# A gated recurrence and a feed-forward block on one core: the first chunk's hand-written order exchanged for another

## The chip, the core and the metric

One Trainium2 chip, one of its cores. A core has TensorE (PE, with weight loads shown as PEld), VectorE (DVE), ScalarE (ACT), GpSimd (POOL) and SyncE (SP), which here issues nearly all DMAs. Each engine runs its own instructions in order and waits on semaphores for the others. The metric is the device time of one execution in microseconds, lower is better.

## The reference

An mLSTM cell over 4 batches x 8 heads x 768 steps with head size 40, then a feed-forward block. At each step, with stabilised input and forget gates `i`, `f`:

```python
C = f * C + i * outer(v, k)        # state, 40 x 40 a head
n = f * n + i * k
y = sigmoid(o) * (C @ q) / max(abs(n @ q), 1)
```

The outputs of all heads are put side by side, `x` of 3072 tokens x 320, and then `out = leaky_relu(x @ w_in, 0.01) @ w_out` with 2048 inner columns. `w_in` and `w_out` come as fp64, all else as fp32.

## The kernel before

The 768 steps are cut in 6 chunks of 128; a chunk has 4 samples (one for each batch), numbered `s` = 4 * chunk + batch. Within a chunk the recurrence is written as attention: scores k q^T, a decay mask's exponential, the product with v, and a state carried on. Then the chunk's 512 tokens go through the feed-forward block.

**Chunk 0 (`first_chunk`)** is ordered by hand. The text `ORDER` is a list of steps with arguments, and each step appends its instructions to the engines' queues in that order (`tc.manual_schedule` keeps it for PE, DVE, ACT and POOL; SP's DMAs follow the order of the calls too). The steps that matter here:

- `warm n`: n matmuls of the identity into a bank that nobody reads, 128x128 fp32. The trace has two records for each.
- `g c`, `ge c`, `ug c`: a chunk's gate sums on DVE (L297 to L317), their exponentials on ACT (L323 to L329), and turning them on PE (`tg`, copied at L357 and L359).
- `ld s`, `lo s`, `fd s`, `ll s i`, `lw n`: loads. `ld` is k, q and v of a sample; `lo` its output gate; `fd` k, v and the decay rows of a sample of chunk 1 (L375, L382, L451); `ll` q or the gate (L422); `lw n` one weight piece, 0 to 3 quarters of `w_in` (each in four requests, L231), 4 and up an eighth of `w_out` (L237).
- `tr s i`, `tc s i`: turn k (0) or q (1) on PE (L586), copy it on ACT (L592). `sc`, `scm`: scores on PE (L601), times the decay on DVE (L608). `ab n`, `abw s`: decay rows of two samples on PE (L472), with the mask on DVE (L482). `exp`: eight exponentials on ACT (L499).
- `vu`, `st`, `stc`: v times gate on POOL (L509), state sum on PE (`dC`, L616), copied on DVE (L624). `val`, `den`, `o`, `gate`, `gp`: values on PE (`pa`, L681), denominators (L673 to L675), tanh on ACT (L534), gating on DVE (L693), scaling on POOL (L710). `x`, `xc`: turn the result (L884) and copy it (L897, L898).
- `nw n e`: the next step of narrowing weight piece n (half e, if given) from fp64 to fp32: a cast on ACT (L264) and six steps on DVE (L266, L268, L270, L275, L279, L281). The last writes the weights that the matmuls read.
- `ff j b0 b1`: one feed-forward unit of some samples (`ph`, L915), with its leaky relu on ACT (L923).
- `tiles`, `ps n`: fills of GpSimd. 

PSUM is 8 banks: 4 for feed-forward and fillers (tag "mm"), 4 for the cell (tag "c"); a step that opens a bank waits for the readers of the one that it takes. SP's DMAs share eight landing semaphores, so an issue waits until the DMA eight places ahead has landed.

**The rest of chunk 0's feed-forward** is a loop over 30 units `ffs[i]`: units 0 and 1 finish the two tiles for samples 2 and 3, 2 to 13 are the other tiles of `x @ w_in` (two units a tile), 14 to 29 multiply by `w_out` (L951; four steps of accumulation for each of 4 samples). Between them:

- `PASSES[i]`: how many steps of the other narrowing (pieces 2 to 11, seven steps each) are put ahead of unit i.
- `fetch`: ahead of which unit a piece of `w_out` is loaded (n = 3 to 7).
- `place`: after which unit the next entry of chunk 1's list of cell work is put: `u_parts` (`sd`, L658 and L663) and `u_plain` (`hN`, L721) of samples 4 to 7, the gates of chunk 2, four turnings.
- `ahead(s)`, called ahead of unit 0 for sample 4 and after each `u_plain` for the next one: turns k and q (`u_split`, PE `tk` at L559, ACT copies at L567), scales q (L527), carries the state (L636) and scales k (`vu`, L519), the last three on POOL.

After these units a planner's table drives chunks 1 to 5; the change doesn't touch it.

Of the kernel before, what the change touches and what calls it, by code (L numbers as in the profile page):

```python
# [22 lines left out]
def kernel(  # L23
# [27 lines left out]
    B, H, S, D = q.shape  # L51
# [25 lines left out]
    gp = ctx.enter_context(tc.tile_pool(name="gates", bufs=1))  # L77
# [67 lines left out]
    def subs(s):  # L145

        for u in range(2):
            yield u, ts(u, SL), slice(SL * (1 - u), SL * (1 - u) + D)
# [212 lines left out]
    st = {}  # L361
# [44 lines left out]
    def padded(s):  # L406

        return rb_t[s % NR][:, 1, : H * DP].rearrange("p (h d) -> p h d", d=DP)
# [8 lines left out]
    def load_late(s, i):  # L417

        if B <= s < 2 * B:
            if i > 0:  # L420
                c, b = divmod(s, B)
                nc.sync.dma_start(natural(s, i), (k, q, o_gate)[i][b, :, ts(c, P), :].rearrange("h p d -> p h d"))  # L422
        elif s < NS:
            load_blocks(s, i)
# [28 lines left out]
    def spread_q(s):  # L453

        c, b = divmod(s, B)
        d = st.setdefault(s, {})
        d["ea"] = late_t[:, s % EAB, :].rearrange("p (h t) -> p h t", t=SL)
        for r in range(2):
            nc.sync.dma_start(
                d["ea"][ts(r, SL)], a_dr[c, 1, 1 - r, b * H : (b + 1) * H, :].partition_broadcast(SL),  # L460
            )
# [24 lines left out]
    def prep_mask(s):  # L486
        if s in masked:
            return
        masked.add(s)
        w = st[s]["w"]  # L490
        nc.gpsimd.tensor_tensor(w, w, cm2.unsqueeze(1).to_broadcast([P, H, SL]), op=ALU.add)  # L491

    def prep_exp(s):

        c, b = divmod(s, B)
        w = st[s]["w"]
        for h in range(H):
            bh = b * H + h
            yield nc.scalar.activation(w[:, h, :], w[:, h, :], AF.Exp, bias=gT[c][:, 0, bh : bh + 1], scale=1.0)  # L499
# [23 lines left out]
    def prep_qs(s):  # L523

        c, b = divmod(s, B)
        d = st[s]
        nc.gpsimd.tensor_tensor(  # L527
            mixed(s)[:, 0, :, :D], natural(s, 1), gT[c][:, 2, ts(b, H)].unsqueeze(2).to_broadcast([P, H, D]), op=ALU.mult,
        )
# [10 lines left out]
    def prep_kq(s):  # L540

        d = st[s]
        d["kqT"] = cw.tile([P, 2, PR * P], F32, name="kqT")
        for i in range(2):
            nc.vector.transpose(
                d["kqT"][:, i].rearrange("p (h t n) -> p h n t", n=TS, t=QW),
                raw_blocks(s, i, QW).rearrange("p (h n) d -> p h n d", n=TS),
            )
        for r in range(2):
            rows = ts(r, SL)  # L550
            nc.vector.tensor_tensor(  # L551
                mixed(s)[rows, 1 - r], d["kqT"][rows, 1].rearrange("p (h t) -> p h t", t=SL), d["ea"][rows], op=ALU.mult,
            )

    def turned(name, src):

        bank = psc.tile([P, PR, P], F32, name=name, tag="c")
        for j in range(PR):
            nc.tensor.transpose(bank[:, j, :], src[:, 2 * j : 2 * j + 2, :].rearrange("p h d -> p (h d)"), ident[:])  # L559
        return bank  # L560

    def to_halves(s, bank, dst):

        for u, toks, rows in subs(s):
            by = dst(u, rows).rearrange("p (j e) t -> p j e t", e=2)
            for e in range(2):
                nc.scalar.copy(by[:, :, e, :], bank[DP * e : DP * e + D, :, toks])  # L567
# [2 lines left out]

        to_halves(s, turned("tq", mixed(s)[:, 0]), lambda u, rows: mixed(s)[rows, u])

    def u_split(s):

        d = st[s]
        d["kqT"] = cw.tile([P, 2, PR * P], F32, name="kqT")
        for i, bank in enumerate([turned("tk0", d["k"]), turned("tk1", padded(s))]):
            to_halves(s, bank, lambda u, rows: d["kqT"][rows, i].rearrange("p (h t) -> p h t", t=SL))

    def u_transpose(s, i):  # L580
        d = st[s]
        if i == 0:
            d["kqT"] = cw.tile([P, 2, PR * P], F32, name="kqT")
        tp = d["tp", i] = psc.tile([P, PR, P], F32, name="tkq", tag="c")
        for j in range(PR):
            nc.tensor.transpose(  # L586
                tp[:, j, :], d["kq"[i]][:, 2 * j : 2 * j + 2, :].rearrange("p h d -> p (h d)"), ident[:],
            )
# [42 lines left out]
    def state_next(s, u):  # L631
        c, b = divmod(s, B)
        rows, old = state_of(s, u)
        _, new = state_of(s, 1 - u)
        g = gL[c][rows, u, ts(b, H)].unsqueeze(2).unsqueeze(3).to_broadcast([D, H, 2, V1])
        nc.gpsimd.tensor_tensor(new, old, g, op=ALU.mult)  # L636
# [442 lines left out]
    def ahead(s):  # L1079

        if s < NS:
            if s < 2 * B:
                u_split(s)
            if s >= 2 * B:
                late[s] = 3
            lazy[s] = prep_exp(s)
            if s < 2 * B:
                prep_qs(s)
            else:
                prep_kq(s)  # L1090
            if s + NR < NS:
                load_late(s + NR, 0)
                load_late(s + NR, 1)
                if s + NR >= 2 * B:
                    spread_q(s + NR)
            state_next(s, 0)
            if s >= 2 * B:
                place_v(s)
            prep_vu(s)
            if s + 1 <= 2 * B:  # L1100
                prep_mask(s + 1)
# [10 lines left out]
            nc.tensor.matmul(st["warm"][:], lhsT=ident[:], rhs=ident[:], start=True, stop=True)  # L1112

    ORDER = """
warm 2; warm 2; g 0; ld 1; ld 0; ge 0; lo 0; ld 2
lw 0; lo 1; warm 6; warm 5; ab 0; ug 0; tr 1 0; tr 0 0
tc 1 0; ld 3; lo 2; tr 0 1; abw 1; abw 0; warm 1; tc 0 1
tc 0 0; tr 1 1; sc 0; warm 3; vu 1; vu 0; lw 1; lo 3
st 0; o 0; tc 1 1; exp 0; scm 0; exp 1; stc 0; st 1
stc 1; warm 5; warm 1; sc 1; warm 6; scm 1; val 0; ab 2  # L1120
g 1; abw 2; abw 3; tr 2 0; tc 2 0; o 1; tr 2 1; val 1
warm 1; tr 3 0; vu 2; ps 1; ge 1; nw 0 0; den 0; gate 1
gate 0; tc 2 1; vu 3; tiles; tc 3 0; exp 2; o 2; warm 5
sc 2; gp 0; den 1; scm 2; nw 0 1; nw 0 0; nw 0 0; ug 1
warm 2; warm 1; nw 0 0; nw 0 1; x 0; tr 3 1; val 2; nw 0 1
warm 4; st 2; xc 0; tc 3 1; exp 3; gate 2; den 2; sc 3
stc 2; gp 1; scm 3; x 1; gp 2; ps 0; fd 4; nw 0 0
nw 0 0; nw 0 1; st 3; ll 4 1; lw 2; warm 5; val 3; nw 0 1
nw 0 0; xc 1; o 3; gate 3; den 3; nw 0 1; nw 0 1; nw 1
nw 1; stc 3; nw 1; ps 3; nw 1; ll 4 2; lw 3; x 2  # L1130
warm 1; ff 0 0 2; gp 3; ps 2; fd 5; ll 5 1; lw 4; x 3
xc 2; xc 3; lw 5; fd 6; fd 7; nw 1; nw 1; ff 1 0 2
ll 5 2; lw 6; nw 1
"""

    def first_chunk():

        ffs, narrow = [], {}

        def ff(j, b0, b1):  # L1140
            if not ffs:
                ffs.extend(ff_units(0))
            ffs[0](j, b0, b1)

        def step(n, e=None):
            if (n, e) not in narrow:
                narrow[n, e] = narrow_weights(n, e)
            next(narrow[n, e], None)

        acts_of = {  # L1150
            "ld": load, "lo": load_o, "lw": load_weights, "g": gates, "ge": gates_exp, "warm": warm,
            "ug": lambda c: gates_T(c, bus[c][0] if c == 0 else bus.pop(c)[0]),
            "tr": u_transpose, "tc": transpose_copy, "ab": lambda n: spread_first(bus[0][1], n), "abw": spread_mask,
            "exp": lambda n: run(prep_exp(n)), "vu": prep_vu, "tiles": prepare_tiles, "sc": u_scores, "scm": scores_mix,
            "st": state, "stc": state_copy, "val": u_values, "den": values_den, "o": prep_o, "gate": gate,
            "gp": gate_scale, "nw": step, "ps": prepare_step, "x": u_x, "xc": x_copy, "ff": ff,
            "warmer": warmer, "idle": idle, "fd": feed, "ll": load_late,
        }
        for line in ORDER.split("\n"):
            for what in line.split(";"):  # L1160
                name, *args = what.split() or [None]
                if name:
                    acts_of[name](*map(int, args))
        return ffs[1]

    E = mybir.EngineType
    with tc.manual_schedule(engines={E.PE, E.DVE, E.Activation, E.Pool}):
        ffs = first_chunk()
        fetch = {1: (3, 4), 16: (7,), 12: (5, 6)}
        PASSES = (6, 0, 3, 0, 3, 3, 0, 3, 0, 2, 1, 0, 5, 1, 11, 0, 1, 3, 3, 3, 1, 12, 2, 3, 4, 0, 2, 1, 2, 21)  # L1170
        place = (1, 6, 11, 12, 16, 18, 19, 20, 22, 23, 25, 25, 26)
        late = {}
        now = (None for n in range(2, QN + NF // 2) for _ in narrow_weights(n))

# [9 lines left out]
        for i in range(len(ffs)):  # L1184
            run(now, PASSES[i])
            for n in fetch.get(i, ()):
# [13 lines left out]
            while done < min(len(cells), sum(p <= i for p in place)):  # L1200
                fn, s = cells[done]
# [7 lines left out]
            while fed < done:  # L1209
                fn, s = cells[fed]  # L1210
# [134 lines left out]
```

## Time and profile before

| | us |
|---|---|
| median of 3 runs | 484.05 |
| lowest, highest | 483.19, 484.30 |
| the profiled execution | 484.15 |
| its span, first to last instruction | 482.3 |
| PE, DVE, ACT, POOL busy | 475.2, 363.9, 199.5, 161.3 |
| first feed-forward matmul starts | 38.91 |
| chunk 1's feed-forward starts | 129.63 |

Times in the trace count from the span's start; what lies around the span is 484.15 - 482.3 = 1.85 us. A row of the timeline gives start, length, engine, line, operation, tiles out<-in, shape and count; in brackets stands how long the engine was idle before it and who released it. Matmul ends are modelled, so TensorE can seem busy while it waits for a short time.

### The profile page before, as it was taken

How to read it: one execution, taken by the hardware profiler on the slowest of the kernel's cores; microseconds unless marked ns; L12 is line 12 of the kernel's file. 1: busy time of each engine (PE TensorE's matmuls, PEld its weight loads, DVE VectorE, ACT ScalarE, POOL GpSimd, SP SyncE). 2: the span in 40 equal slices, each digit the busy share in tenths (PEclk: the TensorE clock that was granted, in tenths of full speed). 3: DMA queues.
4: the chain of work that ended last, by engine and by line, in shares of the span. 5: the costliest groups of instructions: out<-in, count | busy, mean ns of one | idle time of the engine just before them, and what ended most of it. 6: DMA issues, size and time to landing. Idle time of an engine off the chain costs nothing.

```text
span 482.3 us, 12095 instructions
## 1 busy us (share of the span) xinstructions
PE 475.2 (99%) x4757; PEld 373.6 (77%) x4757; DVE 363.9 (75%) x601; ACT 199.5 (41%) x523; POOL 161.3 (33%) x209
## 2 busy tenths in 40 slices
PE   8999999989999999999999999999999999999997
PEld 7998755767655499955569985548998899988997
DVE  4589997999917989877897957889899967335611
ACT  3597875662732332305251222624025642156310
POOL 4056132462602827545641644562310002000020
PEclk9999999999999999999999999999999999999999
DMA  8989868885536676676767968754150030100001
GB/s 146 209 151 223 206 95 246 228 209 123 127 100 130 151 168 168 158 178 175 153 170 161 229 162 207 174 138 121 64 224 31 1 110 0 51 6 1 7 8 41
DMA packets 142599, 63.35 MB, mean 131 GB/s; under 512 B 110480, under 2 KB 130768, under 8 KB 142544
## 3 DMA queue, kind: packets, MB, share of 16 engines
q1 hardware_dynamic: 142160, 62.47, 54.5%
q8 instruction: 37, 0.61, 0.5%
q14 instruction: 18, 0.15, 0.1%
q10 hardware_dynamic: 384, 0.13, 0.1%
HBM read 51.68 MB, written 8.27 MB: 124 GB/s over the span
## 4 chain that ended last, share of the span: by engine, by line
PE 86%; DVE 7%; DMA 2%; SPq 1%; POOL 1%; ACT 1%; issue 1%; POOLq 0%; DVEq 0%
PE po L990 32%; PE ph L915 25%; PE ph L841 8%; PE po L951 4%; PE pe L841 4%; PE pT L751 3%; PE sd L658 3%; PE warm L340 3%; DVE w_out L281 1%; DMA raw<-in_moe_w_out_dram 1%; PE sd L663 1%; DMA S<-in_v_dram 1%; DVE late L270 1%; DVE w_out L279 1%; PE pa L681 1%
## 5 line engine op out<-in xcount | busy, mean ns | idle before, releaser
L915 PE MATMUL ph<-xT,w_in 64*128 64x512 f32 (+1 forms) x680 | 142.4, 569 | 0.4 <-DVE w_in L281 0.3
L915 PEld LDWEIGHTS ph<-xT,w_in 64*128 64x128 f32 x680 | 68.4, 187 | 63.9 <-issue 60.0
L990 PE MATMUL po<-w_out,acts 128*128 128x160 f32 x640 | 90.2, 300 | 0.0
L990 PEld LDWEIGHTS po<-w_out,acts 128*128 128x128 f32 x640 | 87.4, 190 | 1.9 <-ACT w L499 0.8
L923 ACT ACTIVATE acts<-ph 128x512 f32<-128x512 f32 (+1 forms) x68 | 35.1, 567 | 79.1 <-PE ph L915 79.0
L499 ACT ACTIVATE w<-w,gT 128x64 f32<-128x64 f32 (+1 forms) x192 | 51.7, 347 | 28.1 <-POOL w L491 28.1
L636 POOL TENSOR_TENSOR S<-S,f 40x336 f32<-40x336 f32 x36 | 35.0, 973 | 76.5 <-PE pT L751 50.9
L990 PE MATMUL po<-raw,acts 128*128 128x160 f32 x320 | 45.1, 299 | 0.0
L1028 POOL TENSOR_TENSOR y<-y,raw 128x160 f32<-128x160 f32 x10 | 6.3, 633 | 113.3 <-ACT y L1027 113.3
L990 PEld LDWEIGHTS po<-raw,acts 128*128 128x128 f32 x320 | 44.0, 190 | 0.0
L668 DVE TENSOR_TENSOR qn<-w,sd 64x512 f32<-64x512 f32 x40 | 27.4, 685 | 20.5 <-PE sd L663 12.2
L951 PE MATMUL po<-w_out,acts 128*128 128x320 f32 x128 | 36.5, 436 | 0.0
L863 DVE SCALAR_TENSOR_TENSOR acts<-ph,acts 128x512 f32<-128x512 f32 x32 | 20.6, 685 | 20.6 <-ACT acts L861 20.6
L551 DVE TENSOR_TENSOR qn<-kqT,late 64x512 f32<-64x512 f32 x32 | 35.0, 1093 | 1.0
L491 POOL TENSOR_TENSOR w<-w,i 128x512 f32<-128x512 f32 x20 | 31.8, 1588 | 9.3 <-ACT acts L923 9.2
L951 PEld LDWEIGHTS po<-w_out,acts 128*128 128x128 f32 x128 | 23.6, 190 | 9.7 <-issue 0.8
L765 POOL TENSOR_TENSOR xb<-xb,den 128x320 f32<-128x320 f32 x16 | 11.7, 729 | 47.5 <-DVE xb L762 47.5
L861 ACT ACTIVATE acts<-pe 128x512 f32<-128x512 f32 x32 | 17.4, 594 | 18.6 <-PE pe L841 18.6
L769 DVE STREAM_TRANSPOSE x<-xb 128x512 f32<-128x512 f32 x16 | 17.8, 1109 | 7.8 <-POOL xb L765 7.8
L658 PEld LDWEIGHTS sd<-kqT 40*64 40x64 f32 x640 | 19.7, 135 | 5.0 <-issue 4.6
L867 ACT ACTIVATE acts<-acts 128x512 f32<-128x512 f32 x32 | 19.7, 633 | 8.2 <-DVE acts L863 8.2
L990 PE MATMUL po<-raw 128*128 128x160 f32 x160 | 22.8, 300 | 0.0
(167 smaller groups left out, 774.9 us busy)
## 6 DMA issues: line engine op xcount, KB each, us to landing
w<-a_dr SPq DMA_DIRECT2D x40, 128.0 KB, 3.7
rb<-in_k_dram SPq DMA_DIRECT2D x64, 80.0 KB, 2.6
rb<-in_q_dram SPq DMA_DIRECT2D x64, 80.0 KB, 2.5
rb<-in_o_gate_dram SPq DMA_DIRECT2D x64, 80.0 KB, 2.5
xT<-x_dr SPq DMA_DIRECT2D x32, 160.0 KB, 3.4
late<-a_dr SPq DMA_DIRECT2D x32, 128.0 KB, 3.1
x_dr<-x SPq DMA_DIRECT2D x16, 256.0 KB, 2.6
kn<-in_k_dram SPq DMA_DIRECT2D x24, 160.0 KB, 3.8
```

The costliest lines, as they stand in the source:

```text
L491: nc.gpsimd.tensor_tensor(w, w, cm2.unsqueeze(1).to_broadcast([P, H, SL]), op=ALU.add)
L499: yield nc.scalar.activation(w[:, h, :], w[:, h, :], AF.Exp, bias=gT[c][:, 0, bh : bh + 1], scale=1.0)
L551: nc.vector.tensor_tensor(mixed(s)[rows, 1 - r], d["kqT"][rows, 1].rearrange("p (h t) -> p h t", t=SL), d["ea"][rows], op=ALU.mult,)
L636: nc.gpsimd.tensor_tensor(new, old, g, op=ALU.mult)
L658: nc.tensor.matmul(bank[1 - u][toks, h, :], lhsT=kqT[rows, 0, ts(h, SL)], rhs=kqT[rows, 1, ts(h, SL)], start=True, stop=True,)
L668: nc.vector.tensor_tensor(mixed(s)[toks, u], w[toks], bank[1 - u][toks], op=ALU.mult)
L841: nc.tensor.matmul(ph[r][:], lhsT=parts["w", key][n][part, at : at + P], rhs=xs[key][part, slot, :], start=start and slot == 0, stop=stop ...
L863: nc.vector.scalar_tensor_tensor(fs[r], in0=ph[r][:], scalar=1.0 + EPS, in1=fs[r], op0=ALU.mult, op1=ALU.add,)
L915: nc.tensor.matmul(ph[r][:, cols], lhsT=w_row(r, slot, j), rhs=xT[DP * r : DP * (r + 1), slot, bs, :], start=(slot == 0), stop=(slot == KC ...
L923: nc.scalar.activation(acts[:, f, cols], ph[r][:, cols], AF.Prelu, alpha=0.01)
L951: nc.tensor.matmul(po[n][:], lhsT=acts[:, f, ts(n, P)], rhs=w_out[:, f, :], start=(f == 0), stop=(f == NF - 1),)
L990: nc.tensor.matmul(bank[:], lhsT=left[:, f, :], rhs=right[:, f, :], start=f == 0, stop=f == KH - 1)
```

## The change

Four things change, and no arithmetic:

1. `u_split` is cut in two, `split_turn` (PE) and `split_copy` (ACT). For sample 4 they become steps of `ORDER` (`sp 4`, `spc 4`, close to its end), and `ahead` skips them for that sample.
2. `ORDER` is another text: the same steps otherwise, with 44 fillers instead of 50, in another order. On SP, `lw 0` stands ahead of `ld 2`, `lo 3` ahead of `lw 1`, `lw 4` ahead of `fd 5`, and `fd 7` last.
3. `fetch` loads pieces 3 and 4 of `w_out` ahead of unit 3 instead of 1, and 5 and 6 ahead of unit 7 instead of 12.
4. `PASSES` and `place` have other numbers: sample 4's and sample 5's `u_plain` one unit later (7 and 13), sample 6's `u_parts` and `u_plain` one unit earlier (15 and 17), the turnings at 23, 24, 24, 27 instead of 23, 25, 25, 26.

```diff
--- before.py
+++ after.py
@@ -570,12 +570,21 @@
 
         to_halves(s, turned("tq", mixed(s)[:, 0]), lambda u, rows: mixed(s)[rows, u])
 
+    def split_turn(s):
+
+        st[s]["tk"] = [turned("tk0", st[s]["k"]), turned("tk1", padded(s))]
+
+    def split_copy(s):
+
+        d = st[s]
+        d["kqT"] = cw.tile([P, 2, PR * P], F32, name="kqT")
+        for i, bank in enumerate(d.pop("tk")):
+            to_halves(s, bank, lambda u, rows: d["kqT"][rows, i].rearrange("p (h t) -> p h t", t=SL))
+
     def u_split(s):
 
-        d = st[s]
-        d["kqT"] = cw.tile([P, 2, PR * P], F32, name="kqT")
-        for i, bank in enumerate([turned("tk0", d["k"]), turned("tk1", padded(s))]):
-            to_halves(s, bank, lambda u, rows: d["kqT"][rows, i].rearrange("p (h t) -> p h t", t=SL))
+        split_turn(s)
+        split_copy(s)
 
     def u_transpose(s, i):
         d = st[s]
@@ -1079,7 +1088,7 @@
     def ahead(s):
 
         if s < NS:
-            if s < 2 * B:
+            if B < s < 2 * B:
                 u_split(s)
             if s >= 2 * B:
                 late[s] = 3
@@ -1112,25 +1121,25 @@
             nc.tensor.matmul(st["warm"][:], lhsT=ident[:], rhs=ident[:], start=True, stop=True)
 
     ORDER = """
-warm 2; warm 2; g 0; ld 1; ld 0; ge 0; lo 0; ld 2
-lw 0; lo 1; warm 6; warm 5; ab 0; ug 0; tr 1 0; tr 0 0
-tc 1 0; ld 3; lo 2; tr 0 1; abw 1; abw 0; warm 1; tc 0 1
-tc 0 0; tr 1 1; sc 0; warm 3; vu 1; vu 0; lw 1; lo 3
-st 0; o 0; tc 1 1; exp 0; scm 0; exp 1; stc 0; st 1
-stc 1; warm 5; warm 1; sc 1; warm 6; scm 1; val 0; ab 2
-g 1; abw 2; abw 3; tr 2 0; tc 2 0; o 1; tr 2 1; val 1
-warm 1; tr 3 0; vu 2; ps 1; ge 1; nw 0 0; den 0; gate 1
-gate 0; tc 2 1; vu 3; tiles; tc 3 0; exp 2; o 2; warm 5
-sc 2; gp 0; den 1; scm 2; nw 0 1; nw 0 0; nw 0 0; ug 1
-warm 2; warm 1; nw 0 0; nw 0 1; x 0; tr 3 1; val 2; nw 0 1
-warm 4; st 2; xc 0; tc 3 1; exp 3; gate 2; den 2; sc 3
-stc 2; gp 1; scm 3; x 1; gp 2; ps 0; fd 4; nw 0 0
-nw 0 0; nw 0 1; st 3; ll 4 1; lw 2; warm 5; val 3; nw 0 1
-nw 0 0; xc 1; o 3; gate 3; den 3; nw 0 1; nw 0 1; nw 1
-nw 1; stc 3; nw 1; ps 3; nw 1; ll 4 2; lw 3; x 2
-warm 1; ff 0 0 2; gp 3; ps 2; fd 5; ll 5 1; lw 4; x 3
-xc 2; xc 3; lw 5; fd 6; fd 7; nw 1; nw 1; ff 1 0 2
-ll 5 2; lw 6; nw 1
+warm 6; warm 2; warm 2; g 0; ld 1; ld 0; ge 0; lo 0
+lw 0; ld 2; lo 1; warm 5; ab 0; tr 0 0; tr 1 0; tc 1 0
+ld 3; lo 3; lo 2; tr 0 1; abw 0; abw 1; tc 0 1; tc 0 0
+tr 1 1; ug 0; sc 0; vu 0; vu 1; lw 1; warm 5; warm 4
+st 0; st 1; o 0; tc 1 1; exp 0; scm 0; exp 1; stc 0
+sc 1; warm 4; scm 1; stc 1; val 0; ab 2; nw 0 0; g 1
+tr 2 0; val 1; tc 2 0; o 1; tr 2 1; tr 3 0; ps 1; vu 2
+ge 1; abw 2; abw 3; den 1; den 0; gate 1; gate 0; tc 2 1
+tc 3 0; vu 3; exp 2; gp 0; o 2; warm 4; ug 1; sc 2
+scm 2; nw 0 1; nw 0 0; nw 0 0; warm 2; nw 0 0; nw 0 1; x 0
+tr 3 1; val 2; nw 0 1; warm 4; st 2; xc 0; tc 3 1; exp 3
+den 2; gate 2; st 3; sc 3; stc 2; gp 1; gp 2; tiles
+ps 0; fd 4; nw 0 1; nw 0 0; scm 3; x 1; ll 4 1; lw 2
+warm 4; nw 0 0; nw 0 1; warm 2; nw 0 0; xc 1; o 3; val 3
+nw 0 1; gate 3; den 3; nw 1; stc 3; ps 3; ff 0 0 2; ll 4 2
+lw 3; x 2; nw 0 1; nw 1; nw 1; nw 1; gp 3; ps 2
+lw 4; fd 5; ll 5 1; x 3; xc 2; xc 3; lw 5; fd 6
+nw 1; nw 1; nw 1; ff 1 0 2; lw 6; ll 5 2; sp 4; spc 4
+fd 7
 """
 
     def first_chunk():
@@ -1154,7 +1163,7 @@
             "exp": lambda n: run(prep_exp(n)), "vu": prep_vu, "tiles": prepare_tiles, "sc": u_scores, "scm": scores_mix,
             "st": state, "stc": state_copy, "val": u_values, "den": values_den, "o": prep_o, "gate": gate,
             "gp": gate_scale, "nw": step, "ps": prepare_step, "x": u_x, "xc": x_copy, "ff": ff,
-            "warmer": warmer, "idle": idle, "fd": feed, "ll": load_late,
+            "sp": split_turn, "spc": split_copy, "warmer": warmer, "idle": idle, "fd": feed, "ll": load_late,
         }
         for line in ORDER.split("\n"):
             for what in line.split(";"):
@@ -1166,9 +1175,9 @@
     E = mybir.EngineType
     with tc.manual_schedule(engines={E.PE, E.DVE, E.Activation, E.Pool}):
         ffs = first_chunk()
-        fetch = {1: (3, 4), 16: (7,), 12: (5, 6)}
-        PASSES = (6, 0, 3, 0, 3, 3, 0, 3, 0, 2, 1, 0, 5, 1, 11, 0, 1, 3, 3, 3, 1, 12, 2, 3, 4, 0, 2, 1, 2, 21)
-        place = (1, 6, 11, 12, 16, 18, 19, 20, 22, 23, 25, 25, 26)
+        fetch = {7: (5, 6), 16: (7,), 3: (3, 4)}
+        PASSES = (6, 0, 4, 0, 5, 2, 0, 1, 2, 1, 1, 1, 3, 1, 7, 1, 2, 1, 4, 6, 1, 12, 0, 5, 6, 1, 1, 0, 1, 21)
+        place = (1, 7, 11, 13, 15, 17, 19, 20, 22, 23, 24, 24, 27)
         late = {}
         now = (None for n in range(2, QN + NF // 2) for _ in narrow_weights(n))
 
```

More of the change, by code (lines that the diff above doesn't have):

```diff
@@ L571, in split_qs, with u_split @@
         to_halves(s, turned("tq", mixed(s)[:, 0]), lambda u, rows: mixed(s)[rows, u])
-    def u_split(s):
+    def split_turn(s):
+        st[s]["tk"] = [turned("tk0", st[s]["k"]), turned("tk1", padded(s))]
+    def split_copy(s):
         d = st[s]
         d["kqT"] = cw.tile([P, 2, PR * P], F32, name="kqT")
-        for i, bank in enumerate([turned("tk0", d["k"]), turned("tk1", padded(s))]):
+        for i, bank in enumerate(d.pop("tk")):
             to_halves(s, bank, lambda u, rows: d["kqT"][rows, i].rearrange("p (h t) -> p h t", t=SL))
+    def u_split(s):
+        split_turn(s)
+        split_copy(s)
     def u_transpose(s, i):
```

## The prediction

> **What bounds the kernel now.** First the top of the page, then the busy time by stage (columns: PE, PEld, DVE, ACT, POOL busy with counts, PE clock, DMA share, GB/s).
>
> ```profile
> span 482.3 us, 12095 instructions
> ...
> PE 475.2 (99%) x4757; PEld 373.6 (77%) x4757; DVE 363.9 (75%) x601; ACT 199.5 (41%) x523; POOL 161.3 (33%) x209
> ```
>
> ```profile
> 84.35:107.48 23.13, 21.91 (x241) 16.09 (x239) 21.95 (x35) 14.65 (x42) 11.93 (x11) 1.00 0.88 219
> ...
> 129.63:483.00 353.37, 349.33 (x3571) 277.68 (x3570) 252.94 (x400) 115.73 (x301) 106.30 (x128) 1.00 0.45 114
> ```
>
> TensorE is busy for all but 7 us. From 129.63 us to the end the same instructions stand in the same order in both kernels; those 353 us move as a block. So the question is how much earlier TensorE reaches 129.63. After its start at 1.47 it is idle for little, as its waits show (us in total, times, longest):
>
> ```profile
> PE tg L347 <- DVE hn L732: 0.7, 1, 0.7
> ...
> PE sd L663 <- POOL vu L519: 0.5, 1, 0.5
> PE ph L915 <- DVE w_in L281: 0.3, 1, 0.3
> ```
>
> But "busy" hides two things. Ahead of 38.91 it runs 50 fillers (`warm`, matmuls of the identity that nothing reads), which pass time until others are done. And VectorE is almost as full: 21.95 of 23.13 us from 84.35 on. It narrows the fp64 weights, and TensorE waits for it wherever the order lets it fall behind. Three places carry the sum: the end of the front, chunk 0's third weight quarter, and the two stalls after 100 us.
>
> **The change part by part.** Nothing is added to the arithmetic. There are 44 fillers instead of 50; all else is order.
>
> *The front to sample 1's values.* The chain (start, length, what):
>
> ```profile
> 16.41 1.09 PE sc L601 x16
> 17.50 1.53 PE warm L340 x12
> 19.03 1.71 PE pa L681 x16
> 20.75 1.10 PE ab L472 x32
> ...
> 41.93 2.43 PE ph L915 x20
> 44.36 1.02 PE tk L559 x8
> ```
>
> VectorE there (start, length; brackets: idle before, and who ended it):
>
> ```profile
> 14.88 1.29 DVE L608 TENSOR_TENSOR w<-w,sc 128x512 f32<-128x512 f32 x2 [2.75 <-ACT w L499]
> ...
> 21.95 0.28 DVE L305 TENSOR_TENSOR a<-F,m 32x128 f32<-32x128 f32 x1 [2.09 <-PE ab L472]
> ...
> 26.07 1.29 DVE L693 SCALAR_TENSOR_TENSOR x<-acts,pa 128x320 f32<-128x320 f32 x2 [0.35 <-ACT kqT L592]
> ...
> 28.08 1.28 DVE L608 TENSOR_TENSOR w<-w,sc 128x512 f32<-128x512 f32 x2 [0.27 <-ACT w L499]
> ...
> 33.07 0.68 DVE L624 COPY S<-dC 40x168 f32<-40x168 f32 x2 [0.19 <-PE dC L616]
> 34.21 1.29 DVE L608 TENSOR_TENSOR w<-w,sc 128x512 f32<-128x512 f32 x2 [0.46 <-ACT w L499]
> ...
> 40.54 1.24 DVE L281 SCALAR_TENSOR_TENSOR w_in<-w_in,late 128x640 f32<-128x640 f32 x1
> ...
> 42.56 0.68 DVE L624 COPY S<-dC 40x168 f32<-40x168 f32 x2
> ```
>
> The exponentials on ScalarE stand behind the same four copies and one tanh as before, so I leave them where they are; sample 0's mix on VectorE then still ends at 14.88 + 1.29 = 16.17. In the new order that mix frees the banks of sample 1's scores, which start at about 16.17 instead of 16.41: 0.24 earlier. Behind them stand 4 fillers instead of 6; twelve records (six fillers) took 1.53, so one takes 0.255 and two are worth 0.51. Values 0 (1.71) and ab 2 (1.10) follow as now. So L305, which waits for ab 2, goes from 21.95 to 21.2: **0.75 earlier**. If ScalarE were late instead, these 0.75 go; if TensorE could run freely here, all six fillers (1.53) would be won.
>
> *From L305 to the second feed-forward unit.* VectorE takes from 21.95 to 40.54 + 1.24 = 41.78 to reach the end of the first quarter's second half (L281), which `ff 1` waits for; the brackets in between sum to 0.35 + 0.27 + 0.19 + 0.46 = 1.27 idle. The new order holds the same steps. Followed step by step with the durations of the trace, VectorE waits only for the scores of sample 2, about 0.3. The bounds are 0 and 1.27; I take 0.97 won. Against that, the state copy of sample 3 (0.68 at 42.56) now stands ahead of this L281 instead of behind it. So it ends at 41.78 - 0.75 - 0.97 + 0.68 = 40.74, and `ff 1` starts **1.04 earlier**. TensorE is there in time: `ff 0` needs the half that ends 1.72 earlier, at about 37.2, then come 2.43 for `ff 0` and 0.68 for two turnings, 40.3. VectorE itself, with the copy done, is 1.72 ahead.
>
> *The turning of chunk 1's first k and q (tk, 1.02 at 44.36).* On TensorE it stands directly behind `ff 1` in both orders: worth nothing. On ScalarE its eight copies now stand ahead of the cast of quarter 2 instead of behind it; that cast then ends at about 48.7, just when VectorE comes for it (50.70 - 1.72 = 48.98, from the first row below). Nothing gained; if VectorE were earlier still, it would wait there.
>
> ```profile
> 49.21 1.49 DVE L281 SCALAR_TENSOR_TENSOR w_in<-w_in,late 128x1280 f32<-128x1280 f32 x1
> ...
> 58.91 1.48 DVE L281 SCALAR_TENSOR_TENSOR w_in<-w_in,late 128x1280 f32<-128x1280 f32 x1
> ```
>
> ```profile
> 51.59 11.79 PE L915 MATMUL ph<-xT,w_in 64*128 64x512 f32 x52
> ...
> 65.40 10.57 PE L915 MATMUL ph<-xT,w_in 64*128 64x512 f32 x48
> ...
> 84.35 6.73 PE L951 MATMUL po<-w_out,acts 128*128 128x320 f32 x24
> ```
>
> *Third quarter.* 48 passes take 10.57, so 0.22 each; the 52 from 51.59 should take 11.45 and take 11.79. The 0.34 are a wait: after 40 passes (60.4) TensorE stood before quarter 2's L281, which ends at 58.91 + 1.48 = 60.39. New: TensorE is there at 50.55 + 8.8 = 59.35, L281 done at 58.67. The wait goes: **0.34**, and VectorE keeps 0.7 in hand.
>
> *Sample 4's plain part one unit later, samples 5 and 6 shifted.* Here a new wait can arise. VectorE has five steps of w_out's first load ahead of sample 4's gate, and GpSimd's chain behind that gate ends in `vu` of sample 5, which the `sd` matmuls at 76.49 (now 75.1) need:
>
> ```profile
> 65.15 1.94 DVE L281 SCALAR_TENSOR_TENSOR w_in<-w_in,late 128x1280 f32<-128x1280 f32 x1
> ...
> 72.60 1.23 DVE L281 SCALAR_TENSOR_TENSOR w_out<-w_out,xb 128x640 f32<-128x640 f32 x1
> ...
> 77.92 1.40 DVE L668 TENSOR_TENSOR qn<-w,sd 64x512 f32<-64x512 f32 x2 [2.41 <-ACT qn L567]
> ...
> 79.77 0.81 DVE L270 SCALAR_TENSOR_TENSOR late<-w_out,late 128x640 uint16<-128x640 uint16 x1
> 80.50 0.48 DVE L275 TENSOR_SCALAR w_out<-w_out 128x640 uint32<-128x640 uint32 x1
> ```
>
> ```profile
> 68.91 0.74 POOL L710 TENSOR_TENSOR x<-x,den 128x320 f32<-128x320 f32 x1 [3.17 <-DVE x L732]
> ...
> 71.97 1.19 POOL L519 TENSOR_TENSOR vu<-kn,gT 128x320 f32<-128x320 f32 x1
> ```
>
> Quarter 3's L281 ends at 67.09, now 65.37. From there to the end of the load's L281 the trace needs 73.83 - 67.09 = 6.74, gate included; its L281 (1.23) moves behind the gate. So the gate is done by 70.9, GpSimd starts 0.14 later and needs 4 instructions, 68.91 to 73.16, 4.25: 75.3. Late by 0.2 at most, and queued behind it on TensorE is everything. I add **0.2**. In the other direction: VectorE idles 2.41 ahead of 77.92, and two steps that now follow (0.81 and 0.48) are put into that idle time, which gives VectorE 1.3 more lead.
>
> *The two stalls after 100 us.* TensorE waits 0.7 for sample 6's gate and 0.5 for sample 7's `vu` behind it.
>
> ```profile
> 97.03 1.21 PE L721 MATMUL hN<-S,qn 128*64 128x42 f32 x32
> ```
>
> ```profile
> 100.81 0.16 DVE L673 TENSOR_SCALAR den<-hN 128x8 f32<-128x8 f32 x1
> ```
>
> Sample 6's hN ends at 98.24, but VectorE takes up its denominators 2.6 later, at 100.81, because load 8's other steps and two of load 9's stand ahead. In the new order one step of load 8 stands ahead of them and five follow, and the whole part comes one w_out unit earlier (24 passes in 6.73 are three units, 2.24 each). Gate and `vu` then come over 3 us sooner against TensorE than now; both stalls go: **1.22**. What is late next is load 9's L281, about 1 us ahead of its matmul.
>
> *Transfers.* On SP the first quarter's four requests pass sample 2's three loads:
>
> ```profile
> 8.00 0.80 SPq L373 DMA_DIRECT2D kn<-in_k_dram  x1
> ...
> 10.58 2.80 SPq L231 DMA_DIRECT2D acts<-in_moe_w_in_dram  x4
> ```
>
> ```profile
> DMA to landing us min/median/max: 3.2/6.8/7.6
> ```
>
> They are issued 10.58 - 8.00 = 2.58 earlier and land, at 7.6 after the last issue, by 18; the cast that reads them stands behind exponentials that end at 17.5, with 3 us of room to the next turning. Sample 2's loads come about 2.8 later, by 18 to 20.4, and are turned at 21 or later. The loads of w_out that move (4 ahead of sample 5's, 5 and 6 from unit 12 to 7) arrive before their casts. I cost all of it at nothing; each us of lateness at the first cast beyond 20.5 would cost that much.
>
> **Sum:** -1.04 - 0.34 + 0.2 - 1.22 = -2.4 us. The profiled execution took 484.15 us with a span of 482.3, so 481.75; the median of the three runs is 484.05, 0.1 below it, so **481.7**. About 0.2% (1 us) is what a measurement of this kernel can tell from no change.
>
> **Rivals.** *The stalls move instead of going.* GpSimd or VectorE falls behind at sample 5, 6 or 7, since steps on VectorE vary with what GpSimd does beside them (0.48 and 0.82 to 1.3 for like steps). Then 1.22 is lost and 1.2 remain: 482.9. For it: margins of 0 to 1 us. Against: over 3 us at the stalls themselves. 0.17.
>
> *The front gains nothing.* If the first cast or the mixes keep VectorE's pace, and the stalls only shrink, -0.3 to -0.9 remain: about 483.5. 0.11.
>
> *The clock falls (slower).* At the start thirty filler records ran slowly:
>
> ```profile
> 1.47 6.46 PE L340 MATMUL warm<-ident 128*128 128x128 f32 x30 [1.47 <-POOL ident masks.py:199]
> ```
>
> ```profile
> 9.04:12.17 3.13, 0.46 (x2) 1.00 1.12 195
> ```
>
> 6.46 for thirty, against 30 x 0.1275 = 3.83 at the later rate. In the new order the front has four groups of turnings in a row and a wait for the copies, about 9.04 to 11.75, with no matmul at all; if TensorE's clock falls there and is not back until ab 2, its work up to that point (scores 2 x 1.09, fillers 13 x 0.255, values 1.71, ab 1.10, states 0.74) takes twice as long, up to 9.0 us more, of which the waits there absorb little: 484.1 - 2.4 + 9.0 = 490.7. From 2.4 us of such loss on, the kernel is slower. Against it: now from 9.04 to 12.17 the only matmul is one filler (0.46 of 3.13), and what follows runs at full rate. The Trainium skill ("TensorE: Matmul & The Clock Gate", Part 4: PE-mode transpose, and Part 1) says that transposes don't count as busy and that about 3.4 us idle halve the clock; by it 2.7 us would pass, and one window lost would cost some 2.6. The trace's 3.13 us agree that this is short enough. 0.05.
>
> Further unforeseen collisions of queues: 0.07, half of them slower.
>
> **How the numbers follow.** Forecast 0.6, the rivals 0.17, 0.11, 0.05, the rest 0.07. Faster by over 0.2%: 0.6 + 0.17 + a few of the third = 0.79. Within 0.2%: 0.11. Slower: 0.10, the clock and half of the rest, rounded up for what a hand schedule misses. The range: down to 480.2 (all 1.27 idle and all fillers of the front won), up to 483.7 (front without gain); beyond lie the clock and part of the rest.
>
> **What would show it.** `ff 1` at about 40.9, quarter 1's L281 done at 49.0, `sd` of sample 5 near 75.1 with no wait for `vu`, w_out's first unit near 83, no TensorE wait at sample 6's gate, and 129.63 becoming 127.2. Wrong: a TensorE wait over 0.5 on `vu`, or fillers at the slow rate after 9 us.

## The result, and the profile after

Over 12 executions each, the median went from 483.88 us (482.87 to 484.73) to 481.72 us (480.94 to 483.62). The ratio is 0.9966, 95% interval 0.9951 to 0.998: faster by 0.2 to 0.5%. The recorded 481.7 is met, but the 12 executions fall into two groups, and that was not foreseen: seven at 480.94 to 481.74 with a mean TensorE clock of 1.000, five at 483.1 to 483.62 with 0.996. The profiled execution (483.1 us, span 481.1) is one of the five. (Apart from these groups, a few executions of several kernels, of the kernel before too, took several us or far longer, all but one, the 2776.31 of `later_half`, with a mean clock of 0.993 or less; the counts of falls leave them out.) Its page, the totals and the slices:

```profile
span 481.1 us, 12080 instructions
...
PE 474.7 (99%) x4745; PEld 373.6 (78%) x4745; DVE 365.4 (76%) x601; ACT 199.7 (42%) x523; POOL 160.4 (33%) x209
...
PEclk9998999999999999999999999999999999999999
```

The fourth digit of the clock's row, the slice from 36.1 to 48.1 us, is below 9. Cut into the stretches around it (columns as in the prediction's first table; the clock stands third from the end):

```profile
34.26:37.67 3.41, 2.90 (x26) 2.69 (x26) 3.41 (x6) 2.71 (x5) 2.26 (x8) 1.00 0.99 208
37.70:41.11 3.41, 3.41 (x19) 2.91 (x16) 3.28 (x9) 0.00 (x0) 1.90 (x6) 0.50 1.07 223
41.11:44.52 3.41, 3.41 (x29) 2.53 (x28) 3.34 (x4) 3.07 (x9) 3.33 (x3) 1.00 1.18 194
```

From 37.70 to 41.11 us TensorE gets half its clock. The chain there shows what stands in that stretch:

```profile
33.32 1.50 PE L340 MATMUL warm<-ident 128*128 128x128 f32 x12
34.66 2.17 PE L690 MATMUL pa<-S,w 128*128 128x41 f32 x16
37.24 4.12 PE L924 MATMUL ph<-xT,w_in 64*128 64x256 f32 x20 [0.41 <-DVE w_in L281]
...
42.09 2.43 PE L924 MATMUL ph<-xT,w_in 64*128 64x256 f32 x20
```

The first feed-forward unit starts at 37.24, 1.67 earlier than before (38.91), but its 20 passes take 4.12 instead of 2.43, and the second unit starts at 42.09 instead of 41.93. Against the kernel before, TensorE's waits are now these (us in total, times, longest):

```profile
PE sc L610 <- ACT kqT L601: 0.5, 1, 0.5
PE po L960 <- DVE w_out L281: 0.5, 1, 0.5
PE ph L924 <- DVE w_in L281: 0.4, 1, 0.4
```

The two after 100 us are gone, as forecast; a new one of 0.5 stands at w_out (120.3 us), and one of 0.5 at the first scores. The next chunk's feed-forward starts at 128.38 (129.63 before), 1.25 earlier in spite of the lost clock.

The same kernel profiled once more, without a fall (`again`, below; 481.23 us, span 479.3):

```profile
34.17 2.17 PE L690 MATMUL pa<-S,w 128*128 128x41 f32 x16
36.75 2.43 PE L924 MATMUL ph<-xT,w_in 64*128 64x256 f32 x20 [0.41 <-DVE w_in L281]
...
40.12 2.43 PE L924 MATMUL ph<-xT,w_in 64*128 64x256 f32 x20
```

Here the second unit starts at 40.12 and the next chunk's at 126.66, 2.97 ahead of before. Not all of that is the change: executions also differ at their start. The same 18 records of fillers, first in the profiled execution of after, then in `again`:

```profile
4.19 3.51 PE L340 MATMUL warm<-ident 128*128 128x128 f32 x18
```

```profile
4.18 2.33 PE L340 MATMUL warm<-ident 128*128 128x128 f32 x18
```

At 0.213 a record while slow and 0.112 when fast, with 0.16 behind the last, 13 of the 18 were slow in the first (up to 7.0 us) and 1.5 in the second (up to 4.5). The profiled execution of before had its slow rate until 7.5, the latest of all here. So the lengths of stretches are compared, not times from zero. From the PE and ScalarE timelines: the start of sample 0's exponentials (L499), from there to the second feed-forward unit, from that to w_out's first unit, from that to the next chunk's feed-forward:

| kernel (one profile each) | exp. start | to 2nd unit | to w_out | to chunk 1 |
|---|---|---|---|---|
| before | 12.69 | 29.24 | 42.42 | 45.28 |
| after, clock falls | 12.24 | 29.85 | 41.87 | 44.42 |
| again (after, no fall) | 11.76 | 28.36 | 42.10 | 44.44 |
| fill2_again | 12.07 | 28.36 | 42.11 | 44.43 |
| front_half | 11.54 | 29.21 | 42.41 | 45.27 |
| later_half | 11.53 | 29.19 | 42.79 | 44.43 |
| split_only | 12.52 | 29.25 | 42.41 | 45.28 |
| unit6 | 12.04 | 28.37 | 42.10 | 44.42 |
| queue | 11.73 | 29.69 | 42.12 | 44.42 |
| lead | 12.03 | 28.36 | 42.10 | 43.53 |

Behind the last mark every profile takes 352.6 to 352.8 us to the end of its span, but for `later_half` (352.3). At equal start and without a fall, the change is worth 0.88 + 0.32 + 0.84 = 2.0 us in these stretches. The start itself comes 0.2 earlier at most: at the slow rate until 6.64, `fill2_again` has its exponentials at 12.07, where two profiles with the old front, 12.69 at 7.5 and 11.53 at 4.9, put 12.3. But `front_half`, with the new front and the slow rate until 4.9, has 11.54, and `again`, in which TensorE waits 0.63 for the first keys, 11.76.

### The profile page after: what moved, and what is told of

It is laid out like the page before. It is cut to its first block, busy times and chain, and to the rows that moved or that the text cites. A ratio compares the mean times of both kernels' runs of the same rounds, so it can differ in the third digit from the quotient of the medians.

```text
span 481.1 us, 12080 instructions
## 1 busy us (share of the span) xinstructions
PE 474.7 (99%) x4745; PEld 373.6 (78%) x4745; DVE 365.4 (76%) x601; ACT 199.7 (42%) x523; POOL 160.4 (33%) x209
## 4 chain that ended last, share of the span: by engine, by line
PE 90%; DVE 6%; SPq 2%; issue 1%; DMA 1%; ACT 0%; POOL 0%; DVEq 0%; POOLq 0%
PE po L999 32%; PE ph L924 30%; PE ph L850 8%; PE pe L850 4%; PE pT L760 3%; PE sd L667 3%; PE warm L340 3%; PE po L960 2%; PE pa L690 1%; PE sd L672 1%; PE sc L610 1%; SPq L438 1%; DVE w_out L281 1%; DVE w_out L279 1%; PE tkq L595 1%
## 5 line engine op out<-in xcount | busy, mean ns | idle before, releaser
L924 PEld LDWEIGHTS ph<-xT,w_in 64*128 64x128 f32 x680 | 70.9, 190 | 62.8 <-issue 57.8
L499 ACT ACTIVATE w<-w,gT 128x64 f32<-128x64 f32 (+1 forms) x192 | 51.7, 348 | 29.6 <-POOL w L491 29.6
```

The source lines that it names most:

```text
L924: nc.tensor.matmul(ph[r][:, cols], lhsT=w_row(r, slot, j), rhs=xT[DP * r : DP * (r + 1), slot, bs, :], start=(slot == 0), stop=(slot == KC ...
```

## The experiments

The theory: in the thin stretch ahead of the first feed-forward matmul (16 value matmuls of 41 columns and two waits) TensorE does too little, and the clock is halved when one of the windows of 3.41 us, by which the last section finds it granted, falls on that stretch. The rivals: the six missing fillers, the turnings in a row at 9 us, or chance.

**again**: the changed kernel, no edit.

> The changed kernel once more, to count how often its TensorE clock falls, beside the kernels of this call. Theory 1 (thin stretch): ahead of the first feed-forward matmul TensorE runs only 41-wide value matmuls and waits 0.26 and 0.41 us; in those executions in which the unit that grants the clock looks at just that stretch, the clock is halved for 3.4 us and 1.7 us are lost. Then some 5 of 12 executions show a mean clock of 0.996 and about 483.2 us, the others 1.000 and about 481.4. Theory 2 (chance that hangs on no place in this kernel): the kernel before shows such executions as often.

Measured: 482.41 (481.22 to 483.22, 9 executions), 0.9961 of before (0.9947 to 0.9974). Three of 9 at 0.996. With the twelve executions of the result, 8 of 21 fell. The kernel before showed 0.996 in 4 of 61 executions. So it is no mere chance; theory 2 as it stands here falls. The two groups lie 1.8 apart (483.29 and 481.45, medians of the first twelve), more than a fall costs: in the table it is 29.85 - 28.36 = 1.49 at the second unit, of which 0.23 come back (41.87), so 1.3. The rest is the start, which in the profile with the fall comes 0.48 later (12.24 against 11.76); that late starts are those that fall is worked out in the last section. In these nine executions the groups lie closer: 482.76 to 483.22 with a fall, 481.22 to 482.63 without.

**fill2** and **fill2_again**:

```
-... nw 0 0; xc 1; o 3; val 3
+... nw 0 0; xc 1; o 3; val 3; warm 2
```

> Two fillers (0.45 us of TensorE) are put behind sample 3's value matmuls, into the wait of 0.41 us ahead of the first feed-forward matmul. Theory 1 (the thin stretch ahead of the first feed-forward matmul halves the clock): no execution falls, mean clock 1.000 in all, 481.4 to 481.6 us, so about 0.3 less than the changed kernel's median. Theory 2 (the fall comes from the whole front's six fewer fillers, from the turnings in a row at 9 to 11 us, or from chance): still some 4 of 10 executions at 0.996 and about 483.2.

> The changed kernel with two fillers ahead of the first feed-forward matmul, once more, beside the three kernels built on it and for a second count. Theory 1 (the thin stretch alone made the clock fall): no execution with a fall, 481.1 to 482.1 us. Theory 2 (the six executions without a fall were luck): some 4 of 10 at a mean clock of 0.996 and near 483.

Measured: 481.78 (481.09 to 482.03), 0.9947 (0.9934 to 0.996), and 481.72, 0.9943 (0.993 to 0.9956). The medians are that of the changed kernel's first twelve (481.72, seven of which didn't fall), and 0.6 below `again` (482.41). None of the 11 counted executions fell, nor any of the 21 counted of the three kernels built on this one (`queue`, `unit6`, `lead`). The fillers stand where TensorE waited (`fill2_again`):

```profile
34.48 2.17 PE L690 MATMUL pa<-S,w 128*128 128x41 f32 x16
36.48 0.69 PE L340 MATMUL warm<-ident 128*128 128x128 f32 x4
37.10 2.48 PE L924 MATMUL ph<-xT,w_in 64*128 64x256 f32 x20
```

**less**:

```
-... nw 0 1; warm 2; nw 0 0; xc 1 ...
+... nw 0 1; nw 0 0; xc 1 ...
```

> The opposite: two fillers are taken out of the twelve records at 33.3 us, ahead of sample 3's value matmuls. TensorE gets there 0.45 us sooner and waits that much longer for VectorE, so an undisturbed execution stays at 481.4. Theory 1 (thin stretch): the stretch with little work grows by 0.45 of 3.4 us, and the clock falls more often, in 50 to 65% of the executions, about 483.2 us each. Theory 2 (chance, or another place): as often as in the changed kernel.

Measured: 482.21 (481.14 to 482.78), 0.9955 (0.9939 to 0.997). Four of 6 fell, too few to tell from 8 of 21. The profiled one shows the fall at its own place:

```profile
32.83:36.25 3.42, 3.04 (x24) 2.61 (x23) 3.39 (x6) 3.33 (x6) 2.26 (x10) 1.00 0.36 66
36.25:39.66 3.41, 3.10 (x14) 2.74 (x16) 3.28 (x9) 0.09 (x1) 1.92 (x6) 0.50 0.97 235
39.66:43.07 3.41, 3.41 (x31) 2.67 (x28) 3.34 (x4) 2.49 (x7) 3.25 (x4) 1.00 1.08 236
```

The others, 481.14 and 481.27, are as fast as the changed kernel without a fall. A fall costs less here, 0.8 to 1.6, and the four took 482.11 to 482.78 where 483.2 was expected: part of the fall lies on the wait ahead of that matmul (busy 3.10 of 3.41).

**turn**:

```
-... ps 3; ff 0 0 2; ll 4 2
-lw 3; x 2; nw 0 1 ...
+... ps 3; x 2; ff 0 0 2; ll 4 2
+lw 3; nw 0 1 ...
```

> Sample 2's turning (0.33 us of TensorE, three records) is moved from behind the first feed-forward unit into the wait ahead of it, where the kernel before had it. Theory 1 (thin stretch) with turnings that count as work: the stretch is filled much as in the kernel before, no or hardly a fall, clock 1.000, 481.2 to 481.5 us. Theory 1 with turnings that don't count (so the Trainium skill, TensorE: Matmul & The Clock Gate, Part 4: PE-mode transpose): falls in some 4 to 5 of 12 executions, as in the changed kernel. Theory 2 (chance): as in the changed kernel as well.

Measured: 481.88 (481.01 to 486.35), 0.995 (0.993 to 0.997). None of the 11 counted executions fell; the twelfth, 486.35 at a mean clock of 0.993, lost as much as two windows at half the clock take, and where is not known. So turnings fill the stretch as fillers do; the part of the Trainium skill that speaks against it is taken up at the end.

**thin**, the kernel before made thin in the same place:

```
-... lw 3; x 2
-warm 1; ff 0 0 2; gp 3 ...
+... lw 3
+ff 0 0 2; x 2; gp 3 ...
```

> The kernel before, its stretch ahead of the first feed-forward matmul made thin: the filler there is taken out and sample 2's turning moved behind that unit. Theory 1 (a stretch with little TensorE work ahead of that matmul halves the clock when one of the 3.41 us windows falls on it): the clock falls in some 4 of 10 executions (2 of 20 in the kernel before), each about 1.7 us longer, near 486; the others 0.2 to 0.3 over the kernel before, since the turning now stands between the two units. Theory 2 (the changed kernel's falls come from its front as a whole): no more falls than in the kernel before, about 484.3 throughout.

Measured: 484.54 (483.3 to 485.09), 1.0002 (0.9993 to 1.0012). Three of 11 fell, to 484.7, 484.92 and 485.09. More often than in the kernel before (4 of 61), less often than 4 in 10, and dearer by 0.8 rather than 1.7: 484.92 against 484.08, the medians with and without a fall, so near 485, not 486 (none of the three was profiled, so why is open). The executions without a fall aren't 0.2 to 0.3 over the kernel before either. The direction is theory 1's; on 11 executions alone it would not be settled.

**front_half**: the changed kernel with the old `fetch`, `PASSES` and `place`.

> The new first-chunk order with the split turning, and the old later half (passes, places and transfers of the later units as before). Theory 1 (the two halves add up): the front's gain alone, about 1.8 us where the clock doesn't fall (second feed-forward unit at 40.1 against 41.93), the two TensorE waits after 100 us (0.70 and 0.52) stay; so 482.1 without a fall and 483.8 with one, in some 4 of 10 executions. Theory 2 (VectorE's lead from the front already shrinks the two waits): 0.5 to 1.2 less, about 481.2 without a fall.

Measured: 482.9 (four executions at 482.22 to 482.99), 0.9964 (0.995 to 0.9977), none of the four with a fall, and 0.8 over the expected 482.1. Its waits:

```profile
PE tkq L595 <- DMA kn<-in_k_dram: 0.8, 1, 0.8
PE tg L347 <- DVE hn L741: 0.7, 1, 0.7
...
PE sd L672 <- POOL vu L519: 0.5, 1, 0.5
```

The two waits after 100 us stay to the hundredth (45.27 against 45.28 in the table): theory 1. In this one profile the new front isn't faster than the old one (29.21): TensorE waits 0.8 for sample 3's keys, whose load took 5.2 us from issue to landing, against 3.6 in `again`.

**later_half**: the kernel before with the new `fetch`, `PASSES` and `place`.

> The kernel before with only the new passes, places and transfers of the later units. Theory 1 (the halves add up): 0.8 to 1.1 us faster than before, about 483.1; the two TensorE waits after 100 us gone, a new wait of 0.5 for a quarter's last step of w_out, clock 1.000 as in the kernel before. Theory 2 (the later half needs the 1.7 us that VectorE is ahead in the changed kernel): TensorE waits for VectorE at a weight quarter or at sample 5's vu, and the time is within 0.3 of the kernel before, about 484.

Measured: 482.71, 0.9964 (0.9951 to 0.9978), one of 10 fell. The waits:

```profile
PE ph L915 <- DVE w_in L281: 0.8, 2, 0.5
...
PE po L951 <- DVE w_out L281: 0.5, 1, 0.5
```

The two stalls are gone without VectorE's lead, and the new one is there, as theory 1 has it; part is lost at the weight quarters (42.79), and so far theory 2 holds too. The stretches give 0.5 and the end another 0.4, the medians 1.5: some 0.6 of this half's gain isn't accounted for by these marks, and I leave it open. Nor do the medians of the halves add up: each alone is 0.36% under the kernel before, and both together are 0.34 to 0.39% under it. So theory 1's adding up is shown for the two stalls, not for the times.

**split_only**: `sp 4; spc 4` at the end of the old order.

> The kernel before with only the turning of chunk 1's first k and q put at the end of the written order, its copies on ScalarE ahead of the cast of quarter 2. Theory 1 (the turning stands behind the same unit on TensorE, and nobody waits for the copies): no change, within 0.2 us. Theory 2 (the copies, some 1 us earlier, start sample 4's matmuls earlier, or the cast, later by as much, holds VectorE up): 0.3 to 0.5 to one side or the other.

Measured: 483.55, 0.9984 (0.9975 to 0.9993). The median is lower by 0.16%, but all three stretches are those of the kernel before to 0.01, so theory 1 holds in the trace and the 0.16% has no place in it; it may be the spread of the starts, which is not shown.

**queue**, from the kernel with two fillers:

```
-lw 0; ld 2; lo 1; warm 5; ab 0 ...
+ld 2; lo 1; lw 0; warm 5; ab 0 ...
```

> The kernel with two fillers, the four requests for the first weight quarter put back behind sample 2's three loads on SP, as in the kernel before. Theory 1 (the prediction costs that move at nothing): the requests land by 20.4 instead of 17.1, the first cast on ScalarE waits until then, the copy of the next turning behind it comes some 0.1 later: within 0.2 us. Theory 2 (the waiting cast holds up ScalarE, on which sample 2's exponentials stand, and TensorE's scores behind them): 0.5 to 1.0 slower, with a wait of TensorE ahead of its scores or values.

Measured: 482.7 (482.28 to 483.53), 0.9967 (0.9955 to 0.9979): 1.0 slower than the kernel it was made from. Theory 2. On ScalarE the cast waits, and on TensorE the turning behind its copies; sample 2's exponentials, behind the same copies, start at 25.66 (24.45 in `fill2_again`, whose first exponentials come 0.34 later):

```profile
22.32 0.79 ACT L264 ACTIVATE late<-acts 128x640 bf16<-128x640 bf16 x1 [5.80 <-DMA acts<-in_moe_w_in_dram]
23.02 0.57 ACT L601 COPY kqT<-tkq 128x512 f32<-128x512 f32 x1
```

```profile
23.64 0.66 PE L595 MATMUL tkq<-ident,kn 128*128 128x128 f32 x4 [0.55 <-ACT kqT L601]
```

**unit6**, from the kernel with two fillers: `place` with 6 for 7.

> The kernel with two fillers, sample 4's plain part put back from unit 7 to unit 6. Theory 1 (the move itself costs TensorE nothing, since sample 5's vu is there in time either way): within 0.2 us. Theory 2 (the prediction's term: with the part at unit 7, vu of sample 5 comes up to 0.2 late): 0.2 to 0.3 faster than the kernel with two fillers. Theory 3 (with the part at unit 6, VectorE has its denominators ahead of the steps of w_out's first load and waits for hN there): slower by 0.3 to 0.6.

Measured: 481.92 (481.42 to 482.06), 0.9946 (0.9931 to 0.9961), stretches equal to 0.02. Theory 1.

**lead**, from the kernel with two fillers:

```
-PASSES = (6, 0, 4, 0, 5, 2, 0, 1, 2, 1, 1, 1, 3, 1, 7, 1, ...
+PASSES = (6, 0, 4, 0, 5, 2, 0, 1, 2, 1, 1, 1, 3, 2, 6, 1, ...
```

> The same with one narrowing step of VectorE (0.83 to 0.99 us) moved ahead of sample 5's denominators, into the 1.18 us in which VectorE waits there for hN. Theory 1 (from there to 118 us VectorE never waits, so all it does comes 0.8 earlier, and TensorE's wait of 0.48 for a quarter's last step of w_out goes): that wait gone, 0.4 to 0.5 us less than the kernel with two fillers. Theory 2 (VectorE waits somewhere between for another engine, or sample 5's gate, later by up to 0.1, holds up what is behind it): within 0.2 of it, the wait of 0.48 still there.

Measured: 481.1 (nine executions at 480.62 to 482.05, a tenth at 485.06 with a mean clock of 0.993), 0.994 (0.9919 to 0.9961): 0.6 less than the kernel with two fillers, and the fastest of all here. Theory 1, with a little more than it said. VectorE around 81 us, in `fill2_again` first and here second:

```profile
80.37 0.33 DVE L268 TENSOR_SCALAR xb<-xb 128x640 uint16<-128x640 uint16 x1
81.76 0.17 DVE L682 TENSOR_SCALAR den<-hN 128x8 f32<-128x8 f32 x1 [1.06 <-PE hN L730]
```

```profile
80.28 0.33 DVE L268 TENSOR_SCALAR xb<-xb 128x640 uint16<-128x640 uint16 x1
80.64 0.83 DVE L270 SCALAR_TENSOR_TENSOR xb<-raw,xb 128x640 uint16<-128x640 uint16 x1
81.71 0.17 DVE L682 TENSOR_SCALAR den<-hN 128x8 f32<-128x8 f32 x1 [0.24 <-PE hN L730]
```

L270 (0.83) went into the wait for hN. The wait for w_out's L281 is gone (TensorE, the same two):

```profile
118.91 3.50 PE L960 MATMUL po<-w_out,acts 128*128 128x320 f32 x12 [0.48 <-DVE w_out L281]
```

```profile
114.83 6.63 PE L960 MATMUL po<-w_out,acts 128*128 128x320 f32 x24
```

The last stretch takes 43.53 instead of 44.43: 0.9 less, of which 0.75 lie in the 24 passes around that wait (7.21 to 6.46 us from their start to the next turning), though its record shows only 0.48.

## Why the prediction came out right, and where it was wrong

The marks that it named: the second unit at 40.9 (42.09 with the fall, 40.12 without), w_out near 83 (83.96, 82.22), the next chunk at 127.2 (128.38, 126.66). Between them, step by step:

**The front to sample 1's values (-0.75).** Measured from the exponentials, L305 came at 9.26 before (12.69 to 21.95) and 8.66 after (11.76 to 20.42 in `again`): -0.60. The two fillers gave what they should; the scores of sample 1 took 1.31 instead of 1.16. The exponentials, which I left in place, came 0.2 sooner at most, and not in every profile: the four turnings no longer wait for VectorE's mask, but the start can wait for the first keys instead, 0.63 in `again`.

**From L305 to the second unit (-0.29: 0.97 won, 0.68 given).** To the end of that L281, 19.83 became 19.55 in `again`: -0.28. The longest idle of VectorE in it is the 0.34 before sample 2's mix, as forecast. With the two terms `ff 1` is 0.88 earlier from the exponentials and 0.9 to 1.1 in all; the prediction had 1.04.

**The third quarter (-0.34): right in size, wrong in cause.** The wait before quarter 2's L281 did not go. In `again` it stands at its old place, 0.17 long:

```profile
58.70 4.56 PE L924 MATMUL ph<-xT,w_in 64*128 64x512 f32 x20 [0.17 <-DVE w_in L281]
```

VectorE never got the lead of 0.7 over TensorE: its L281 of quarter 1 ends 8.77 after `ff 1` before (50.70 - 41.93) and 8.76 in `fill2_again` (49.19 - 40.43). The state copy of 0.68 is out of that stretch, but L268 takes twice as long, beside a multiply of GpSimd that now begins earlier against it. That the multiply is the cause is read from the overlap alone. VectorE before and in `fill2_again`, then GpSimd in the same order:

```profile
42.56 0.68 DVE L624 COPY S<-dC 40x168 f32<-40x168 f32 x2
43.27 0.74 DVE L268 TENSOR_SCALAR late<-late 128x1280 uint16<-128x1280 uint16 x1
```

```profile
41.06 1.44 DVE L268 TENSOR_SCALAR late<-late 128x1280 uint16<-128x1280 uint16 x1
...
47.70 1.49 DVE L281 SCALAR_TENSOR_TENSOR w_in<-w_in,late 128x1280 f32<-128x1280 f32 x1
```

```profile
42.26 1.40 POOL L491 TENSOR_TENSOR w<-w,i 128x512 f32<-128x512 f32 x1
```

```profile
40.76 1.40 POOL L491 TENSOR_TENSOR w<-w,i 128x512 f32<-128x512 f32 x1
```

What won 0.32 is the place of sample 5's part, one unit later, at the border between w_in and w_out: the 20 passes and both turnings take 4.49 + 1.06 + 0.93 = 6.48, where before 12 passes, hN and turnings, and 8 passes took 2.78 + 1.06 + 1.02 + 1.92 = 6.78. One interruption of the stream fewer is 0.3. TensorE there, before and in `again`:

```profile
77.57 2.85 PE L915 MATMUL ph<-xT,w_in 64*128 64x512 f32 x12
80.35 1.13 PE L721 MATMUL hN<-S,qn 128*64 128x42 f32 x32
...
82.43 1.99 PE L915 MATMUL ph<-xT,w_in 64*128 64x512 f32 x8
```

```profile
75.73 4.56 PE L924 MATMUL ph<-xT,w_in 64*128 64x512 f32 x20
80.22 1.13 PE L730 MATMUL hN<-S,qn 128*64 128x42 f32 x32
...
82.22 4.47 PE L960 MATMUL po<-w_out,acts 128*128 128x320 f32 x16
```

`front_half`, with the old place, takes the same 6.78 there (76.38 to 83.16). That the size came out as forecast is luck.

**Sample 4's part one unit later (+0.2).** No wait of `sd`(5) for `vu` came, and `unit6` is the same time. The 0.2 was my bound for a wait that had room.

**The two stalls (-1.22).** Both went (`front_half` keeps them, `later_half` loses them). I had named what is late next, a load's L281 "about 1 us ahead of its matmul". It is not load 9's but load 11's, and it is 0.48 late; the stretch gained 0.84, not 1.22.

**Transfers (nothing).** Right for the order as it is: nobody waits for the loads that were moved back. The one new wait in the front, 0.8 for sample 3's keys in the one profile of `front_half`, is for a load that kept its place. What the prediction did not say is that the order needs the move, since it has the first cast earlier than before. Undone (`queue`), the cast begins only at 22.32, and it costs 1.0, because the cast stands ahead of the turnings' copies and of sample 2's exponentials on ScalarE. The prediction had a price for a first cast after 20.5, each us that much; this one comes 1.8 after it and costs 1.0.

**The clock.** The rival was right that the clock can fall where TensorE does too little, and wrong in the kind of work, the place and the price: at 9 to 12 us, with turnings and no matmul, nothing happened, and the fall at 37.7 costs 1.3 to 1.5 in 8 of 21 executions, not 9.0. I had looked for stretches without matmuls and not for one with narrow ones. One window at half the clock takes 3.41 us and can lose no more than half of it, 1.7, so the 2.6 that the prediction names for one window lost was too much as well. Without the fall the sum was -2.4, and so is the difference of the medians (483.88 to 481.45, the seven without a fall); the stretches give 2.0, the start 0.2 at most, and where the other 0.2 to 0.4 lie is open. With the falls the median lands on 481.72. The agreement with 481.7 to 0.02 is partly luck.

## What to carry to other kernels

Fillers that "pass time" may also hold the clock: before some are taken out, look at what each 3.4 us of TensorE would then contain, matmul by matmul with its width, and put fillers into the waits that are there anyway. Where several profiles are compared, compare stretches between marks, since the start alone moves by over a microsecond. When a wait goes, look up the next full engine on that path: one step moved into an idle time of VectorE 37 us ahead gave 0.6 us.

## What the runs showed of the hardware

**The clock is granted in windows of 3.41 us that run through.** In the profiled execution of after the slow rate ends at 7.0 and the fall begins at 37.70: 30.7 later, nine times 3.41; it lasts one such time. In `less` the trace's record of the clock has 5.53 and 36.25, the same 30.7. So it would be the start that decides who falls (the changed kernel has one profile with a fall and one without): with the slow rate ending at 4.5, as in `again`, the windows end at 35.2 and 38.6, and the thin stretch (34.2 to 36.8) is divided between two of them. The Trainium skill ("TensorE: Matmul & The Clock Gate", Part 1) has the same: a free-running window of about 3.4 us, and half the clock after an idle window. The trace agrees with the length. It differs on "idle": in the window before the fall TensorE was counted busy for 2.90 of 3.41 us (table above). By columns it did much less: 0.37 of fillers, 16 values at 0.112 x 41/128 = 0.57 and 0.46 of feed-forward are 1.4 of 3.41, 0.41. In the window before the fall of `less` it is 0.70 of fillers and 0.57, 0.37. In `fill2_again`, whose window ends at 37.36 by the same count, it is 0.53 of fillers, 0.57, 0.45 of the two new fillers and 0.26 of feed-forward, 0.53, and the clock stayed. These shares are estimates, which count a 41-column matmul for 41/128 of a filler; the bound would lie between 0.41 and 0.53. Idle time alone doesn't decide it: TensorE was busy for 2.90 and 3.02 of the 3.41 us before these two falls, and for only 2.43 (`again`, 7.92 to 11.33) and 2.57 (`thin`, 35.98 to 39.40) in windows behind which the clock stayed.

**Turnings count.** In `again`, whose windows end at 4.5 + 3.41 n, the one from 7.92 to 11.33 holds turnings and hardly a matmul (0.23 of the scores):

```profile
8.35 1.09 PE L595 MATMUL tkq<-ident,kn 128*128 128x128 f32 x8 [0.63 <-DMA kn<-in_k_dram]
9.28 1.04 PE L595 MATMUL tkq<-ident,qn 128*128 128x128 f32 x8
10.25 0.30 PE L347 MATMUL tg<-ident,bu 32*128 32x32 f32 x2
11.10 1.16 PE L610 MATMUL sc<-kqT 40*128 40x128 f32 x16 [0.55 <-ACT kqT L601]
```

The clock stayed at full. The same page (Part 4: PE-mode transpose) says that transposes don't count as busy in the same way; here the measurement decides, and `turn` (no fall in 11, against 8 of 21) says the same. The trace records these turnings as matmuls, two records each like a filler, and doesn't show whether they run in the transpose mode that the page speaks of.
